# Seven half-width products for eight in an out-projection, with the block sums on GpSimd and inverse sums kept in PSUM

## The chip, the cores and the metric

One core of one Trainium2 chip. The metric is the device time of one execution in microseconds. The trace's span is shorter than that time (246.8 against 248.62 us in the profiled run of the kernel before); times inside an execution are us from the span's start. A run is called slow when its time is over 1.5% above the fastest of the same kernel; ratios use fast runs alone.

## The reference, cut to what matters

```python
# q, k, v: [8, 8, 576, 64], p: [8, 8, 32, 64], w_in: [512, 2048], w_out: [2048, 512]
def sm_attn(qq, kk, vv):                      # softmax(scale q k^T) v
    ...
p_packed = sm_attn(p, k, v)                   # 32 packed rows per head
x = sm_attn(q, p_packed, p_packed)            # -> 4608 tokens x 512
h = x @ w_in
out = (h * np.cos(h)) @ w_out                 # the last product is the out-projection
```

Each of eight batches has 576 tokens: four row blocks of 128 and a half block of 64. Two batches share a fifth block ("joint").

## The kernel before: the parts that the change and the argument touch

One batch is a phase. Its *attention part* computes both softmaxes; its *slot* computes 16 hidden-layer blocks (`h_mm`). Out-projection matmuls of the batch before are a *filler* that `fill(n)` strews between both, so that TensorE never waits for the softmax or for the cosine.

```python
A = ctx.enter_context(tc.tile_pool(name="psA", bufs=3, space=PSUM))   # scores, sums, hidden blocks
O = ctx.enter_context(tc.tile_pool(name="psO", bufs=2, space=PSUM))   # out-projection

def recips(b):                      # two tiny VectorE operations, [128, 2]
    V.reciprocal(r1[b], sums1[b])
    V.tensor_scalar(out=rs1[b], in0=r1[b], scalar1=scale, scalar2=None, op0=ALU.mult)

def sums2(b, y):                    # softmax sums; their logarithm goes to SBUF, which frees psA at once
    if b not in lns:
        lns[b] = att_pool.tile([128, 2, S], FP32, name="lns", tag="lns")
    ps = psa()
    ...                             # two matmuls with ones
    ACT.activation(out=lns[b][:, y]..., in_=ps[:, :, 0:HS], func=AF.Ln)

def h_mm(b, fc):                    # hidden block fc: matmuls, cosine on ScalarE, product on VectorE
    ps = psa()
    ...
    def rest():
        V.tensor_tensor(out=gT[b][:, fc, :]..., in0=ps[:, :, 0:HS], in1=csv, op=ALU.mult)
        if fc % 8 == 7:
            G.tensor_copy(out=joint[b // 2]..., in_=gT[b][:, fc - 7:fc + 1, 512:576])
    return rest

def out_gen(b):                     # 16 matmuls of 512 columns for each row block
    for grp in groups:
        pss = {c: O.tile([128, DM], FP32, name="ot", tag="ot") for c in grp}
        ...
                nc.tensor.matmul(pss[c], w, w_out_bf[:, fc, :], start=(fc == 0), stop=(fc == NFC - 1))
                if fc == NFC - 1:
                    osb = o_pool.tile([128, DM], FP32, name="osb")
                    copy(out_eng[n_out[0] % len(out_eng)], osb, pss[c])

for s in range(3, B):               # attention part, then slot
    fill(1000); set_filler(s - 1)
    if nxt: permute_v(s + 1)        # GpSimd
    s2(s); ppw(s, 2, V); ...
    recips(s + 1)
    xbar("k", s + 2)                # transposing DMA of k
    G.tensor_copy(out=gate, in_=xT["k", s + 2][0:1, 0, 0:1])   # GpSimd waits here until k is transposed
    ...
    for n, b in (("v", s + 2), ("q", s + 2), ("k", s + 3)):
        load(n, b)                  # issued by GpSimd, behind the gate
    slot(s, ...)
```

The softmax here doesn't subtract the row's maximum and nothing guards it: scores larger than these inputs give would overflow.

## Time and profile before

Median 248.38 us of two runs (248.23 to 248.54). The table is worked out from the trace's list of TensorE instructions; a phase runs from the first hidden block of one slot to that of the next.

| | before |
|---|---|
| busy TensorE / VectorE / ScalarE / GpSimd, share of the span | 94 / 67 / 68 / 23 % |
| slot 1 starts, slot 2 starts | 44.2, 77.6 us |
| phases from slot 2 on | 26.1, 25.2, 28.4, 25.2, 28.1 us (64 or 80 whole matmuls of filler in turn) |
| slot 7, then the tail to the end of the span (246.8 us) | 13.4, 22.8 us |

TensorE is full; the others have a third or more of their time free. A change that removes TensorE work should therefore gain, as long as what it puts on the other engines fits between.

### The profile page before, as it was taken

The page shows a single profiled execution, that of the slowest core. Times are in us where ns is not written, and L with a number is a line of the kernel's source. Part 1 is how long each engine was busy: PE and PEld are TensorE (multiplying, and loading weights), DVE is VectorE, ACT ScalarE, POOL GpSimd, SP SyncE. Part 2 cuts the span into 40 slices and gives each one's busy share as a digit, 9 for nine tenths or more (in the row PEclk, how much of TensorE's full clock was granted, in tenths as well). Part 3 has the DMA queues.
Part 4 walks back from the last instruction along what each step waited for, and adds up shares of the span by engine and source line. Part 5 has one row for each costly group of instructions (what it writes and reads, how often), then busy time and mean ns, then how long its engine had stood idle before and what let it go on. Part 6 is the DMA issues. An engine that isn't in the chain of part 4 may idle for free.

```text
span 246.8 us, 5023 instructions
## 1 busy us (share of the span) xinstructions
PE 233.2 (94%) x1996; PEld 130.9 (53%) x2029; DVE 165.2 (67%) x248; ACT 169.0 (68%) x282; POOL 57.7 (23%) x70
## 2 busy tenths in 40 slices
PE   8788799999999999999999999999999999999993
PEld 3454374566545654565446554565456554665452
DVE  3549987677658776678767766678766684886110
ACT  2369799877576787888787776888778684873000
POOL 8342533240400355004503105030500100001000
PEclk9999999999999999999999999999999999999999
DMA  6999999999899999999999997999571113111133
GB/s 90 202 203 206 205 206 228 194 241 151 179 202 184 192 175 214 218 198 142 222 211 187 172 201 91 198 166 171 109 154 27 45 43 84 43 31 57 47 84 85
DMA packets 64231, 37.36 MB, mean 151 GB/s; under 512 B 36848, under 2 KB 59632, under 8 KB 64208
## 3 DMA queue, kind: packets, MB, share of 16 engines
q0 software_dynamic: 23152, 18.75, 50.0%
q1 hardware_dynamic: 40624, 18.09, 35.1%
q8 instruction: 16, 0.26, 0.4%
q10 hardware_dynamic: 432, 0.20, 0.4%
q14 instruction: 7, 0.06, 0.1%
HBM read 37.22 MB, written 9.44 MB: 189 GB/s over the span
## 4 chain that ended last, share of the span: by engine, by line
PE 78%; DMA 12%; issue 2%; DVE 2%; ACT 2%; POOL 2%; DVEq 0%; POOLq 0%
PE ot L309 46%; PE psA L256 21%; DMA vbf<-in_v_dram 10%; PE psA L207 3%; DMA a1T<-a 2%; PE psA L129 2%; PE psA L183 2%; DVE gT L263 2%; PE ot L295 1%; PE psA L233 1%; ACT cosT L260 1%; POOL vp L77 1%; ACT ppT L75 1%; POOL kbf L84 1%; PE ot L104 0%
## 5 line engine op out<-in xcount | busy, mean ns | idle before, releaser
L309 PE MATMUL ot<-w_out_bf,gT 128*128 128x512 bf16 x482 | 127.5, 379 | 2.0 <-issue 1.1
L263 DVE TENSOR_TENSOR gT<-psA,cosT 128x576 bf16<-128x576 f32 x128 | 93.8, 755 | 28.9 <-ACT cosT L260 28.2
L260 ACT ACTIVATE cosT<-psA 128x576 bf16<-128x576 f32 x128 | 82.4, 652 | 24.6 <-PE psA L256 22.1
L256 PE MATMUL psA<-a2n,PPW 128*128 128x288 bf16 x512 | 83.8, 286 | 1.6 <-DVE gT L263 0.4
L309 PEld LDWEIGHTS <-gT 128*128 128x128 bf16 x512 | 47.8, 98 | 43.4 <-issue 6.7
L256 PEld LDWEIGHTS <-PPW 128*128 128x128 bf16 x512 | 49.3, 98 | 34.6 <-issue 3.9
L77 DVE CAST PPW<-psA 128x1024 bf16<-128x1024 f32 (+1 forms) x23 | 26.9, 1175 | 11.6 <-PE psA L207 11.5
L267 POOL COPY joint<-gT 128x512 bf16<-128x512 bf16 x16 | 9.9, 616 | 82.5 <-DVE gT L263 82.5
L77 DVE COPY osb<-ot 128x512 f32<-128x512 f32 (+1 forms) x22 | 14.9, 678 | 17.5 <-PE ot L309 7.7
L77 POOL COPY vp<-vbf 96x3072 bf16<-96x3072 bf16 x7 | 19.3, 2751 | 6.3 <-DMA vbf<-in_v_dram 6.3
L75 ACT COPY osb<-ot 128x512 f32<-128x512 f32 (+1 forms) x15 | 8.5, 567 | 15.3 <-PE ot L309 10.6
L243 DVE SCALAR_TENSOR_TENSOR a2n<-a2u,r,lns 128x576 bf16<-128x576 bf16 x16 | 12.3, 812 | 7.3 <-ACT lns L241 7.3
L235 ACT ACTIVATE lns<-psA 128x576 f32<-128x576 f32 x16 | 10.1, 650 | 7.1 <-PE psA L233 6.5
L140 ACT ACTIVATE a<-psA 128x576 bf16<-128x576 f32 x16 | 10.3, 647 | 6.7 <-PE psA L129 6.7
L309 PE MATMUL ot<-w_out_bf,joint 128*128 128x512 bf16 x47 | 12.8, 379 | 0.1
L225 ACT ACTIVATE a2u<-psA,rs 128x576 bf16<-128x576 f32 x16 | 11.0, 737 | 1.4 <-PE psA L129 1.3
L75 ACT CAST ppT<-psA 64x128 bf16<-64x128 f32 x24 | 6.2, 260 | 7.0 <-DVE ppT L77 5.9
L207 PE MATMUL psA<-w_in_bf,ppT 64*32 64x512 bf16 x224 | 10.1, 380 | 0.0
L241 ACT ACTIVATE lns<-lns 128x576 f32<-128x576 f32 x16 | 10.0, 676 | 0.0
L347 PE MATMUL ot<-wz 128*128 128x512 bf16 x23 | 7.7, 468 | 1.4 <-DVE wz L358 1.2
L527 POOL COPY gate<-kT 1x1 bf16<-1x1 bf16 x3 | 0.5, 181 | 32.3 <-DMA kT<-kbf 32.3
L183 PEld LDWEIGHTS <-vp 96*128 96x128 bf16 x192 | 6.5, 98 | 2.3 <-issue 1.2
(73 smaller groups left out, 152.7 us busy)
## 6 DMA issues: line engine op xcount, KB each, us to landing
kbf<-in_k_dram POOLq DMA_DIRECT2D x8, 576.0 KB, 12.6
vbf<-in_v_dram POOLq DMA_DIRECT2D x8, 576.0 KB, 7.6
qbf<-in_q_dram POOLq DMA_DIRECT2D x8, 576.0 KB, 10.1
out_dram<-osb SPq DMA_DIRECT2D x24, 192.0 KB, 2.7
out_dram<-osb SPq DMA_DIRECT2D x22, 128.0 KB, 2.4
w_in_bf<-in_moe_w_in_dram POOLq DMA_DIRECT2D x4, 512.0 KB, 17.3
w_out_bf<-in_moe_w_out_dram POOLq DMA_DIRECT2D x4, 512.0 KB, 21.2
out_dram<-osb SPq DMA_DIRECT2D x26, 64.0 KB, 2.1
```

Source lines behind the costliest of these rows:

```text
L75: ACT.copy(out=out, in_=in_)
L77: eng.tensor_copy(out=out, in_=in_)
L140: ACT.activation(out=a1[b % 2][:, y, :, 0:TP].rearrange("p (e m) x -> p e m x", e=2), in_=ps[y][:, :, 0:HS].rearrange("p e (m x) -> p e m ...
L183: nc.tensor.matmul(ps[:, hp * 64:(hp + 1) * 64], vp[b][:, c, hp * 128:(hp + 1) * 128], a1T[b][0:TP, :, j, 32 * hp:32 * hp + 32], start=(j ...
L207: nc.tensor.matmul(ps[y][32 * x:32 * x + 32, :], ppT[b % 2][r, 2 * x + y, :], w_in_bf[r, x, n * 512:(n + 1) * 512], start=True, stop=True)
L225: ACT.activation(out=a2u[b][:, y].rearrange("p (e x) -> p e x", e=2), in_=ps[y][:, :, 0:HS], func=AF.Exp, scale=rs1[b][:, y:y + 1])
L235: ACT.activation(out=lns[b][:, y].rearrange("p (e x) -> p e x", e=2), in_=ps[:, :, 0:HS], func=AF.Ln)
L243: V.scalar_tensor_tensor(out=a2n[b][:, y], in0=a2u[b][:, y], scalar=r1[b][:, y:y + 1], in1=lns[b][:, y], op0=ALU.mult, op1=ALU.mult)
L256: nc.tensor.matmul(ps[:, e, 0:HS], PPW[b][:, y, fc * 128:(fc + 1) * 128], a2n[b][:, y, e * HS:(e + 1) * HS], start=(y == 0), stop=(y == 1))
L260: ACT.activation(out=csv, in_=ps[:, :, 0:HS], func=AF.Sin, bias=PI_HALF)
L263: V.tensor_tensor(out=gT[b][:, fc, :].rearrange("p (e x) -> p e x", e=2), in0=ps[:, :, 0:HS], in1=csv, op=ALU.mult)
L309: nc.tensor.matmul(pss[c], w, w_out_bf[:, fc, :], start=(fc == 0), stop=(fc == NFC - 1))
```

## The change

Two row blocks of 128 tokens and the two halves of `w_out` (even and odd hidden chunks, left and right columns) form a 2 by 2 block product. It has eight block products; with sums of blocks formed beforehand and results added afterwards, seven suffice. A matmul of 512 columns is called a *whole*, one of 256 a *half*. Two row blocks together are a *pair*. The sums of `w_out` blocks (T) are formed once, those of the token blocks (S) for each batch.

```diff
+    def T_sums(i, eng):                       # 4 sums of 2048 elements, on VectorE in slot 1
+        in0, in1 = ((B_blk(0, 1), B_blk(0, 0)), (B_blk(1, 1), T[0]), ...)[i]
+        eng.tensor_tensor(out=T[i], in0=in0, in1=in1, op=ALU.subtract)
+    def S_sums(b, p, eng, k0, k1, which=(0, 1, 2, 3)):
+        for i in which:                       # S1 = A21+A22, S2 = S1-A11, S3 = A11-A21, S4 = A12-S2
+            eng.tensor_tensor(out=out, in0=in0, in1=in1, op=op)
+    def pairs_gen(b):                         # replaces the whole matmuls of batches 1 to 7
+        m = {1: (A11, B_blk(0, 0)), 2: (A12, B_blk(1, 0)), 3: (S4, B_blk(1, 1)),
+             4: (A_blk(b, 2 * p + 1, 1, 0, 8), T[3]), 5: (S1, T[0]), 6: (S2, T[1]), 7: (S3, T[2])}
+        ...                                   # 8 matmuls of 256 columns each
+            V.tensor_tensor(out=out, in0=in0, in1=one, op=ALU.add)      # results added out of PSUM
     def slot(s, hooks, keep=0, heavy={}):
         for fc in range(NFC):
             h_mm(s, fc)()
+            if s > 1 and fc in (7, 11):
+                S_sums(s, 0, G, *((0, 4) if fc == 7 else (4, 6)))
+    def close(s, steps=(0, 1)):
+        eng = V if s == B - 1 else G          # the other sums; the last batch's on VectorE
+        ...
     def sums2(b, y):
-        ACT.activation(out=lns[b][:, y]..., in_=ps[:, :, 0:HS], func=AF.Ln)
+        ps = lns[b, y] = psa()                # inverse sums stay in PSUM until the normalising product
+        ACT.activation(out=ps[:, :, 0:HS], in_=ps[:, :, 0:HS], func=AF.Ln)
 for s in range(3, B):
-        fill(1000); set_filler(s - 1)
+        close(s - 1, (0,))                    # S of pair 0 (rest), S1 and S2 of pair 1
         if nxt: permute_v(s + 1)
         ...                                   # gate, loads
+        close(s - 1, (1,))                    # S3 and S4 of pair 1, behind the gate and the loads
         slot(s, ...)
```

The change also has one buffer for the permuted v where there were two, and three for output tiles where there were four.

## The prediction

> **What bounds the kernel now.** I read the page first: busy shares, the chain that ended last, the costliest groups.
>
> ```profile
> PE 233.2 (94%) x1996; PEld 130.9 (53%) x2029; DVE 165.2 (67%) x248; ACT 169.0 (68%) x282; POOL 57.7 (23%) x70
> ...
> PE 78%; DMA 12%; issue 2%; DVE 2%; ACT 2%; POOL 2%; DVEq 0%; POOLq 0%
> ...
> L309 PE MATMUL ot<-w_out_bf,gT 128*128 128x512 bf16 x482 | 127.5, 379 | 2.0 <-issue 1.1
> L263 DVE TENSOR_TENSOR gT<-psA,cosT 128x576 bf16<-128x576 f32 x128 | 93.8, 755 | 28.9 <-ACT cosT L260 28.2
> L256 PE MATMUL psA<-a2n,PPW 128*128 128x288 bf16 x512 | 83.8, 286 | 1.6 <-DVE gT L263 0.4
> ...
> L267 POOL COPY joint<-gT 128x512 bf16<-128x512 bf16 x16 | 9.9, 616 | 82.5 <-DVE gT L263 82.5
> L77 DVE COPY osb<-ot 128x512 f32<-128x512 f32 (+1 forms) x22 | 14.9, 678 | 17.5 <-PE ot L309 7.7
> L77 POOL COPY vp<-vbf 96x3072 bf16<-96x3072 bf16 x7 | 19.3, 2751 | 6.3 <-DMA vbf<-in_v_dram 6.3
> ```
>
> TensorE carries the chain; the out-projection (L309) is its largest group and waited only 2.0 us in all. GpSimd is nearly empty. Busy times of pipelined matmuls overlap, so I took the pitch from two stretches of the chain in order of time where TensorE does nothing else:
>
> ```profile
> 228.37 10.74 PE ot L309 x49
> 239.16 3.67 PE ot L295 x32
> ```
>
> A 512-column matmul (379 ns alone) costs (10.74 - 0.379) / 48 = 215.9 ns; a 256-column one (272 ns alone), with a weight load for each, costs (3.67 - 0.272) / 31 = 109.6 ns. A half is thus 1.6 ns dearer than half a whole, and its 98 ns weight load is just hidden. Last, the busy time by stretch. One batch is a phase of two parts: attention work with out-projection matmuls between it, then a slot of 16 hidden-layer blocks with more of them. Batch 6:
>
> ```profile
> core 0: us, PE busy (x) PEld busy (x) DVE busy (x) ACT busy (x) POOL busy (x), PEclk, DMA share, GB/s
> 182.70:202.20 19.50, 19.28 (x158) 11.48 (x162) 13.93 (x18) 14.60 (x25) 0.77 (x2) 1.00 0.16 44
> 202.20:210.80 8.60, 8.55 (x70) 3.95 (x71) 5.30 (x6) 5.11 (x8) 0.46 (x1) 1.00 0.24 61
> ```
>
> The first line is slot 6, the second the attention part after it. TensorE is full in both, at clock 1.00. VectorE has 5.6 us left in the slot, and that reserve is what the change spends.
>
> **What the Trainium skill says.** (1) "TensorE: Matmul & The Clock Gate", Back-to-back issue gap, gives two figures: an isolated gap of N/2.4 + 2.5 ns and a sustained 131 ns per 512 columns. The trace agrees with the first (216 against 215.9, 109 against 109.6) and not with the second. (2) "GPSIMD Engine Reference", section 3.1, gives about 2.6 cycles at 1.2 GHz per element of a two-input operation and 4497 ns for 2048 fp32 elements. No two-input GpSimd row exists here. Its copies agree with the page's one-input rate: (2751 - 616) / (3072 - 512) = 0.83 ns an element, one cycle. (3) "VectorE: DVE Perf Modes", the perf-mode tier table, gives 1224 ns for a bf16 tensor_tensor of 2048 elements in SBUF; no row here has that form. (4) "SBUF - State Buffer", Who interferes with whom, says that a VectorE instruction with two SBUF inputs contends with GpSimd reads. The old normalising product has two; with the inverse sums in PSUM it has one. The old product takes 812 ns against 755 of the gating product that reads PSUM, so at best 0.06 us each are gained besides the freedom from contention.
>
> **The change part by part.**
>
> *Products.* Each of batches 1 to 7 had 64 whole matmuls for its four row blocks, 13.82 us; now 112 halves, 12.28 us. 7 x 1.54 = 10.8 us saved. The shared fifth blocks of batches 1, 3 and 5 become halves: 96 x 109.6 against 48 x 215.9, 0.16 us lost. Net on TensorE: -10.6 us, all of it on the path as long as TensorE stays fed.
>
> *Sums on GpSimd, batches 1 to 6.* Per batch twelve operations of 512 elements and eight of 256: 8192 elements. Estimate from the skill's 2.6 cycles (2.17 ns an element) and 0.1 us an instruction: 12 x 1.21 + 8 x 0.66 = 19.8 us. To it come the v permutation 2.75, two joint copies 1.2, three load issues 2.3 and a gate 0.5: 26.5 us a batch. TensorE's own phase: the phases starting at 129.0, 157.4 and 182.7 took 28.4, 25.3 and 28.1 us with 80, 64 and 80 whole matmuls; with 128 halves (14.0 us) in each that is about 25.2. So at the skill's rate GpSimd is the longer one, by about 1 us a phase; at 1.9 ns an element (24 us) it would fit. It also has deadlines: the v permutation comes behind the sums, ready about 12.5 us into a phase, and the next use of it (sixth block of the slot) comes at about 13.3 us.
>
> *Evacuations.* Per batch VectorE and ScalarE had 4 or 5 copies of 690 or 581 ns, half on each. Now VectorE does nearly all: per pair two 512-column operations (0.69) and three of 256 (0.42) = 2.64 us, twice, plus about two copies of 0.42: 6.1 us against 1.7 before. Its phase grows from 19.2 (13.93 + 5.30) to about 23.5 of 25.2 us. In the slot, with the ten halves held back, TensorE has 64 halves 7.0 + 16 blocks of 0.49 + 1.4 of other matmuls = 16.2 us, and VectorE 13.2 + about 3 = 16.2 us as well. Neither can lend the other time, and the hidden blocks rotate through three PSUM buffers. I put 0.5 us of slip on each of six slots: +3 us.
>
> *Weight sums in slot 1.* Four VectorE operations of 1.22 us (skill) = 4.9 us in a stretch of 7.3 us in which VectorE is busy 6.4. Most can be absorbed by buffers and by the attention part that follows: +1.5 to +2 us.
>
> *Last batch.* All its sums are on VectorE and stand in its queue before the evacuations: four of 256 elements (about 0.25) and eight of 512 (about 0.4) = 4.2 us. The last gated block is ready about 1.4 us after the slot; with one evacuation between, VectorE reaches the second bank's evacuation at 6.4 us and frees it at 7.1, while TensorE has done its 10 + 8 + 16 + 8 halves by 4.7 us. Stall about 2.3 us; this eats the last batch's 1.5.
>
> *Normalising product.* Queued behind evacuations, its second half comes with only six halves (0.66 us) of cover: up to +0.2 us a phase, +1 in all.
>
> *Sum.* -10.6 + 3 + 1.8 + 2.3 + 1 = -2.5 us with GpSimd just fitting; GpSimd at the skill's rate adds 2 to 5 us over four phases but shares them with the VectorE slip. With everything hidden but the tail stall: about -8 us.
>
> **The rivals.**
>
> *A: TensorE stays the bound.* For it: it is full now, and the ordering of the change (halves of GpSimd sums interleaved, products split, evacuations arranged so that two go in one instruction) looks arranged around exactly these waits. Against it: the VectorE balance of the slot. It gives 248.4 - 8 to -6 = 240 to 242 us.
>
> *B: VectorE becomes the bound of the slots.* For it: 16.2 against 16.2 us and three rotating buffers. Against: before, VectorE's idle time was almost only waiting for ScalarE (28.2 of 28.9 us), and part of its work can slide into the attention part, which has 3 us of reserve. It gives 244 to 246 us.
>
> *C: GpSimd becomes the bound.* For it: 26.5 us of work per phase of 25.2. Against: the rate is a figure for fp32 that nothing here has tested for bf16, and every sum was put there on purpose. It gives 247 to 251 us.
>
> *D: transfers.* Loads are issued behind the sums on the same queue. Before, the gate for them opened 13.4 us after the phase began (133.4 against about 120), held by the transposes of k and not by GpSimd, so a queue that arrives at 13 us loses little. I give it no time of its own.
>
> **Range and chances.** I weigh A at about 0.45, B at 0.35 and C at 0.2. My sum alone would say 246; I lean towards A, since a wait that I counted fully may be covered by TensorE's other matmuls, and because the reordering is so specific. I choose 243.4 us, range 239.5 to 249.0. The 2% limit is 243.4, so faster by over 2% has 0.46, within 2% 0.44, slower 0.10.
>
> **What would show it.** Right: a half-width pitch near 110 ns in the out-projection; GpSimd tensor_tensor rows near 1.2 us for 512 elements and its busy time near 175 us; VectorE busy near 190 us; phases of 25 to 26 us; a stall of about 2 us on TensorE just after the last slot, ended by VectorE. Wrong: if the sums on GpSimd take 0.8 us or less, C falls and A gains; if they take 1.5 us or more, TensorE will wait for S tiles in each phase and the kernel is slower. If the slots run at TensorE's pace with VectorE over 95% busy, my 3 us there were not real. If weight loads show at the 256-column pitch (over 115 ns), the saving itself is smaller: each ns costs 0.9 us.

## The result, and the profile after

The changed kernel takes 268.42 us (267.89 and 268.95, two runs): 8% slower, and outside the predicted range. The ratio to before is 1.0806, 95% interval 1.071 to 1.0903. A ratio here is the mean time of one kernel's fast runs over that of the other's in the same rounds, so it is not quite the ratio of the medians quoted.

The page of the changed kernel: busy times, then the chain that ended last by engine and by line.

```profile
PE 233.7 (87%) x2407; PEld 170.7 (64%) x2413; DVE 200.3 (75%) x327; ACT 164.6 (62%) x278; POOL 177.1 (66%) x198
...
POOL 28%; PE 20%; DVE 7%; DMA 6%; ACT 3%; issue 2%; POOLq 0%; DVEq 0%; ACTq 0%
POOL S L303 23%; PE ot L412 11%; DMA kT<-kbf 6%; PE psA L262 4%; DVE gT L269 4%; PE ot L322 3%; DVE osb L371 2%; ACT cosT L266 2%; POOL joint L273 2%; POOL vbf L87 1%; POOL qbf L87 1%; DVE S L303 1%; ACT ppT L78 1%; PE psA L209 1%; PE psA L186 1%
```

TensorE led the chain with 78%; now GpSimd does with 28%, most of it in the block sums (L303). Yet no engine is full: the fullest is TensorE with 87%. So the loss must lie in waits and not in a saturated engine. TensorE's busy time has not fallen, partly because some of its matmuls ran at half clock (mean granted clock 0.977; h1 below, which has these products in batches 2 to 7 and ran at clock 1.00, has 228.0 us).

Groups of the changed kernel, different shapes kept apart, and last the gate of the kernel before:

```profile
L303 POOL TENSOR_TENSOR S<-gT 128x512 bf16<-128x512 bf16 x38 | 43.4, 1155 | 0.0
L303 POOL TENSOR_TENSOR S<-gT 128x256 bf16<-128x256 bf16 x26 | 17.4, 670 | 0.0
L155 DVE TENSOR_SCALAR rs<-r 128x2 f32<-128x2 f32 x8 | 6.1, 765 | 0.3
L661 POOL COPY gate<-kT 1x1 bf16<-1x1 bf16 x3 | 0.5, 182 | 10.6 <-DMA kT<-kbf 10.6
```

```profile
L527 POOL COPY gate<-kT 1x1 bf16<-1x1 bf16 x3 | 0.5, 181 | 32.3 <-DMA kT<-kbf 32.3
```

The sums take 1155 and 670 ns, where 1.21 and 0.66 us were predicted. The gate is the surprise: GpSimd, the busiest helper of the change, stood 10.6 us in three waits for the transposed k. The wait was there before, 32.3 us long, when GpSimd had nothing else to do and it cost nothing. And a scaling of two elements takes VectorE 765 ns on average.

Where the time came from, phase by phase (starts of the slots' first hidden blocks; experiments included for later):

| kernel | slot 1 | 2 | 3 | 4 | 5 | 6 | 7 | slot 7 ends | span |
|---|---|---|---|---|---|---|---|---|---|
| before | 44.2 | 77.6 | 103.6 | 128.9 | 157.3 | 182.5 | 210.6 | 224.0 | 246.8 |
| after | 49.0 | 87.0 | 115.3 | 141.6 | 167.8 | 201.2 | 227.1 | 242.4 | 267.2 |
| e3_before_psum_only | 48.5 | 83.4 | 108.9 | 134.2 | 162.6 | 187.8 | 215.9 | 229.3 | 252.1 |
| e2_ln0_sbuf | 44.3 | 84.8 | 113.0 | 139.1 | 165.3 | 196.7 | 222.6 | 237.8 | 264.1 |
| e4_sums_before_gate | 48.1 | 86.1 | 114.3 | 140.4 | 166.6 | 192.7 | 218.6 | 233.9 | 260.1 |
| i2_after_b1 | 48.6 | 84.0 | 110.9 | 137.0 | 163.1 | 190.3 | 216.2 | 231.5 | 256.3 |
| g1_all2 | 44.4 | 87.8 | 116.1 | 142.2 | 168.3 | 194.5 | 220.4 | 235.6 | 258.7 |
| g2_small_evac | 44.3 | 87.8 | 114.2 | 138.7 | 164.3 | 189.9 | 215.1 | 229.6 | 251.2 |
| h1_full_b1 | 44.7 | 78.6 | 106.2 | 132.3 | 158.5 | 184.6 | 210.5 | 225.7 | 248.8 |
| i1_h1_small | 44.5 | 78.4 | 104.6 | 130.1 | 155.7 | 181.2 | 206.5 | 220.9 | 242.6 |

Against before, the change loses 4.8 us up to slot 1, 4.6 more up to slot 2, 2.2 up to slot 3, 1.1 up to slot 4 and 8.2 in the phase of slot 5 (33.4 us against 25.2); slot 7 and the tail bring 3.9 more. Only two phases gain, those of slots 4 and 6, by 2.2 us each. Three places in the trace show most of it. The 4.6 us up to slot 2 are lost in attention part 2 (19.9 us against 15.8; slot 1 itself takes 18.1 against 17.6): TensorE waits there 1.4 us for VectorE, 1.2 for a joint copy and 0.6 for block sums.

**Before slot 1.** VectorE's instructions in the prologue, of the kernel before:

```profile
26.59 0.15 DVE L151 RECIPROCAL r<-sums 128x2 f32<-128x2 f32 x1
26.77 0.17 DVE L152 TENSOR_SCALAR rs<-r 128x2 f32<-128x2 f32 x1
```

and of the changed one, with GpSimd's copy of v at the same time (start, duration):

```profile
28.70 0.16 DVE L154 RECIPROCAL r<-sums 128x2 f32<-128x2 f32 x1
28.89 3.10 DVE L155 TENSOR_SCALAR rs<-r 128x2 f32<-128x2 f32 x1
```

```profile
29.20 2.76 POOL L80 COPY vp<-vbf 96x3072 bf16<-96x3072 bf16 x1
```

Batch 0's inverse sums now hold two of the three psA buffers, so TensorE's transposes of k for batch 1 follow one another through the one left. First the kernel before, then two of the three groups after:

```profile
17.54 1.40 PE L104 MATMUL psA<-ident,kbf 96*128 96x96 bf16 x24
```

```profile
19.29 0.50 PE L107 MATMUL psA<-ident,kbf 96*128 96x96 bf16 x8 [0.65 <-DVE kT L80]
20.44 0.50 PE L107 MATMUL psA<-ident,kbf 96*128 96x96 bf16 x8 [0.65 <-DVE kT L80]
```

The scaling comes about 2 us later than before. There it meets GpSimd's copy and ends with it, at 31.96 to 31.99 us: 3.10 us for what took 0.17. (It starts 0.31 us ahead of the copy, while GpSimd still issues a load; in e3 below it starts inside the copy.) TensorE then waits 2.95 us for a gated product, and its next 8 hidden-layer matmuls run at half clock.

**The cycle through the gate.** The chain of waits of the changed kernel in order of time (start, us):

```profile
162.91 6.38 POOL S L303 x7
169.29 0.29 POOL vp L80
169.59 6.78 DMA kT<-kbf
...
176.41 0.18 POOL gate L661
...
176.65 0.79 POOL vbf L87
...
178.22 4.49 POOL S L303 x4
182.71 0.56 POOL joint L273
```

GpSimd forms sums, permutes v, waits at the gate (here 4.44 us idle) for k's transposition, issues the loads and only then forms the last four sums, 4.5 us, which are ready to be formed all the while. The gate opens at 118.33, 146.83 and 176.41: 28.5 and 29.6 us apart, while TensorE's phases take 26.2. GpSimd falls behind by 2.2 to 3.4 us a phase, unnoticed, until TensorE meets it. The transposing DMA itself starts later in each phase too: 2.2 us before slot 3's start, 0.1 before slot 4's, 1.8 after slot 5's. It stands in SyncE's queue behind the transposition of q and output stores. What delays it was not tested.

TensorE's instructions there (start, duration, in brackets the idle time before and what ended it):

```profile
187.27 1.03 PE L322 MATMUL ot<-w_out_bf,joint 128*128 128x256 bf16 x8 [0.46 <-DVE osb L371]
191.07 1.89 PE L322 MATMUL ot<-w_out_bf,joint 128*128 128x256 bf16 x8 [2.76 <-POOL joint L273]
```

TensorE waits 2.76 us for a copy of 0.61 us that stands in GpSimd's queue behind sums which nobody needs yet. Then eight matmuls take 1.89 instead of 1.03 us: the clock has halved, and stays so to 197 us (mean granted clock 0.77 from 186 to 201 us). The Trainium skill, "TensorE: Matmul & The Clock Gate", Part 1, tells of a halved clock after an idle window of about 3.4 us; here it followed idle stretches of 0.46 and 2.76 us with 1.03 us of work between them.

**After the last slot**, TensorE in the changed kernel:

```profile
242.74 1.04 PE L412 MATMUL ot<-w_out_bf,S 128*128 128x256 bf16 x8
246.38 1.92 PE L412 MATMUL ot<-w_out_bf,gT 128*128 128x256 bf16 x16 [2.60 <-DVE osb L371]
```

This stall of 2.60 us is close in length to the 2.3 us that the prediction worked out, but it is not the same stall: it comes right after the halves held back from batch 6, where the prediction had 32 halves of the last batch in between. VectorE there:

```profile
243.94 0.71 DVE L303 TENSOR_TENSOR S<-gT 128x256 bf16<-128x256 bf16 x1
...
245.91 0.94 DVE L371 TENSOR_TENSOR osb<-ot,osb 128x256 f32<-128x256 f32 x2
246.77 0.75 DVE L303 TENSOR_TENSOR S<-gT 128x512 bf16<-128x512 bf16 x2
```

The evacuation that frees the bank, one of batch 6's last, stands behind the four sums of 256 elements alone (243.94 to 245.38 us). The eight sums of 512 follow it, and TensorE waits for none of them. The second line of TensorE also tests the predicted pitch: (1.92 - 0.272) / 15 = 109.9 ns a half, predicted 109.6.

### The profile page after: what moved, and what is told of

Read it like the earlier page. It is cut to its first block, busy times and chain, and to the rows that moved or that the text cites. A ratio compares the mean times of both kernels' runs of the same rounds, so it can differ in the third digit from the quotient of the medians.

```text
span 267.2 us, 6076 instructions
## 1 busy us (share of the span) xinstructions
PE 233.7 (87%) x2407; PEld 170.7 (64%) x2413; DVE 200.3 (75%) x327; ACT 164.6 (62%) x278; POOL 177.1 (66%) x198
## 4 chain that ended last, share of the span: by engine, by line
POOL 28%; PE 20%; DVE 7%; DMA 6%; ACT 3%; issue 2%; POOLq 0%; DVEq 0%; ACTq 0%
POOL S L303 23%; PE ot L412 11%; DMA kT<-kbf 6%; PE psA L262 4%; DVE gT L269 4%; PE ot L322 3%; DVE osb L371 2%; ACT cosT L266 2%; POOL joint L273 2%; POOL vbf L87 1%; POOL qbf L87 1%; DVE S L303 1%; ACT ppT L78 1%; PE psA L209 1%; PE psA L186 1%
## 5 line engine op out<-in xcount | busy, mean ns | idle before, releaser
L266 ACT ACTIVATE cosT<-psA 128x576 bf16<-128x576 f32 x128 | 81.6, 654 | 28.4 <-PE psA L262 24.9
L262 PEld LDWEIGHTS <-PPW 128*128 128x128 bf16 x512 | 49.6, 98 | 26.4 <-issue 12.5
L303 POOL TENSOR_TENSOR S<-gT 128x512 bf16<-128x512 bf16 (+1 forms) x64 | 60.8, 958 | 0.0
L412 PE MATMUL ot<-T,S 128*128 128x256 bf16 x336 | 48.9, 273 | 2.2 <-POOL S L303 2.0
L412 PEld LDWEIGHTS <-S 128*128 128x128 bf16 x448 | 43.1, 98 | 10.8 <-POOL S L303 2.8
L412 PE MATMUL ot<-w_out_bf,gT 128*128 128x256 bf16 x224 | 34.5, 281 | 3.1 <-DVE osb L371 3.1
L303 POOL TENSOR_TENSOR S<-S,gT 128x512 bf16<-128x512 bf16 (+1 forms) x32 | 30.4, 958 | 1.6
L303 POOL TENSOR_TENSOR S<-gT,S 128x512 bf16<-128x512 bf16 (+1 forms) x32 | 30.4, 958 | 0.0
L322 PE MATMUL ot<-w_out_bf,joint 128*128 128x256 bf16 x128 | 16.6, 282 | 6.1 <-POOL joint L273 3.9
L412 PE MATMUL ot<-T,gT 128*128 128x256 bf16 x112 | 16.8, 272 | 1.1 <-DVE osb L371 1.0
L344 PE MATMUL ot<-w_out_bf,gT 128*128 128x512 bf16 x60 | 16.4, 379 | 0.4 <-issue 0.3
L412 PE MATMUL ot<-w_out_bf,S 128*128 128x256 bf16 x112 | 15.8, 272 | 0.0
```

The costliest lines, as they stand in the source:

```text
L262: nc.tensor.matmul(ps[:, e, 0:HS], PPW[b, fc // 4][:, y, fc % 4 * 128:fc % 4 * 128 + 128], a2n[b][:, y, e * HS:(e + 1) * HS], start=(y == ...
L266: ACT.activation(out=csv, in_=ps[:, :, 0:HS], func=AF.Sin, bias=PI_HALF)
L303: eng.tensor_tensor(out=out, in0=in0, in1=in1, op=op)
L322: nc.tensor.matmul(ps, joint[b // 2][:, fc, :], w_out_bf[:, fc, cols], start=(fc == 0), stop=(fc == NFC - 1))
L344: nc.tensor.matmul(pss[c], gT[b][:, fc, c * 128:(c + 1) * 128], w_out_bf[:, fc, :], start=(fc == 0), stop=(fc == NFC - 1))
L412: nc.tensor.matmul(tile_[:, i], lhs[:, kp, :], rhs[:, kp, :], start=kp == 0, stop=kp == 7)
```

## The experiments

Eighteen runs. The theory after reading the two traces was that the loss is a sum: GpSimd's queue (G in the expectations), held PSUM buffers, VectorE's evacuations and the tail. The rival was that one of them carries it alone, GpSimd's added work above all.

### GpSimd's queue

**e1_free_sums** (wrong result): no block sums in batches 1 to 6; the products read plain blocks.

```diff
-        if (b, p) not in S:
+        if (b, p) not in S and b == B - 1:
+        if b < B - 1:
+            return
```

> The changed kernel without the block sums of batches 1 to 6: their products read blocks of gT directly, so GpSimd has no sums there. The result is wrong on purpose; all matmuls, evacuations and the last batch's sums stay. Theory G (GpSimd falls behind, 28.5 us a batch against 26.2 us of TensorE, and TensorE pays where it catches up): the 8.1 us lost in the phase from 167.8 to 201.2 go, and 2 to 3 us of waits for S and joint in the second batch's attention part; 256 to 259 us. Rival V (VectorE is the bound of the slots): at most 2 us less, 266 to 268 us.

Measured: 261.81 us, ratio 1.0521 (1.049 to 1.0553), 6.6 us below the change. One of its four runs took 582 us, and that was the profiled one; its hidden-layer matmuls took 576 ns on average against 289 in the change, so its trace tells nothing of the waits. The gain fell short of what was expected: with no sums at all, two thirds of the loss remain. GpSimd is one cause of several.

**e4_sums_before_gate**: nothing but the place of the last four sums, ahead of the gate instead of behind the loads.

```diff
+            close(s - 1, (1,))
             if s + 2 < B:
                 xbar("k", s + 2)
                 G.tensor_copy(out=gate, in_=xT["k", s + 2][0:1, 0, 0:1])
...
-        close(s - 1, (1,))
         slot(s, ...)
```

> The changed kernel with the last two sums of the second pair placed in GpSimd's queue ahead of the gate that waits for the transposed k, not behind the loads. Theory G, refined: GpSimd stands idle 2.8 to 4.4 us a batch at that gate while 4.5 us of sums wait behind it; filled, its batch falls from 28.5 to about 25.5 us, it keeps up, and the 8.1 us wait at 187 to 191 us with the half clock after it goes: 259 to 262 us. Rival: the rate of the sums is the bound, not their order: 266 us or more. Loads start about 1 us later, which should not matter.

Measured: 261.61 us, ratio 1.053 (1.0477 to 1.0582), the same as with no sums at all. The phase of slot 5 takes 26.2 instead of 33.4 us. GpSimd's waits from 100 to 200 us, first of the change, then of this run (total us, times, longest):

```profile
POOL gate L661 <- DMA kT<-kbf: 10.6, 3, 4.4
```

```profile
POOL gate L663 <- DMA kT<-kbf: 0.2, 1, 0.2
```

With the same work, GpSimd hardly waits: the sums fill the time of the transposing DMA. So in the phases from slot 2 on it was the order of GpSimd's work that cost 6.8 us, and not its amount: TensorE does not wait for GpSimd there any more. The two waits in attention part 2 (1.2 and 0.6 us) are unchanged.

### Inverse sums in PSUM

**e3_before_psum_only**: the kernel before with this one part of the change.

```diff
-            lns[b] = att_pool.tile([128, 2, S], FP32, name="lns", tag="lns")
-        ps = psa()
+        ps = lns[b, y] = psa()
...
-        ACT.activation(out=lns[b][:, y]..., in_=ps[:, :, 0:HS], func=AF.Ln)
+        ACT.activation(out=ps[:, :, 0:HS], in_=ps[:, :, 0:HS], func=AF.Ln)
```

> The kernel before with this part of the change alone: inverse sums in PSUM in all batches, the product not split. Theory P: slot 1 starts 2 us later by the lack of PSUM buffers, up to 4.7 us if the small VectorE operation meets the GpSimd copy again; later batches keep their length. 250 to 253 us. Rival: the loss at the start comes from other parts of the change (buffers merged, order of loads), 248 to 249 us.

Measured: 254.05 us, ratio 1.022 (1.0189 to 1.0252), correct. One part, meant as a small gain for VectorE, costs 5.7 us alone. The table shows where: 4.3 us up to slot 1, 1.5 more up to slot 2, nothing later. VectorE and TensorE in this run:

```profile
29.65 2.19 DVE L152 TENSOR_SCALAR rs<-r 128x2 f32<-128x2 f32 x1
```

```profile
32.56 2.08 PE L255 MATMUL psA<-a2n,PPW 128*128 128x288 bf16 x8 [2.04 <-DVE gT L262]
```

The scaling is again caught by the copy of v (29.05 to 31.81 us), and TensorE idles 2.04 us and then runs at half clock (eight matmuls in 2.08 us; undisturbed blocks of four start 0.49 us apart).

**e2_ln0_sbuf**: the change with batch 0's inverse sums in SBUF.

```diff
+        if b == 0:
+            if y == 0:
+                ln0.append(s_pool.tile([128, 2, SQ], FP32, name="lns0", tag="S1"))
+            lns[b, y] = ln0[0][:, y].rearrange("p (e x) -> p e x", e=2)
...
```

> The changed kernel with the inverse sums of batch 0 alone in SBUF as before; those of the other batches stay in PSUM. Theory P (two of three PSUM buffers held in the prologue make transposes of k wait for one, and the 2 us of delay push a small VectorE operation into a GpSimd copy that blocks it): slot 1 starts at 44.4 us again instead of 49.0 and the time falls by 4 to 5 us, to about 264. Rival G: GpSimd's queue sets the later pace whatever the start, since it waits for transfers; the gain is lost again and the time stays above 267.

Measured: 265.59 us, ratio 1.0693 (1.0666 to 1.0721). Slot 1 starts at 44.3 us, so the prologue's 4.7 us are recovered in full; but slot 2 starts only 2.3 us earlier than in the change. 2.8 us are left of the gain: in attention part 2 TensorE now waits 2.7 us for a joint copy, where it waited 1.2.

### Weight sums, tail and scaling

**f1_T_early**: the four weight sums still on VectorE, two in attention part 1, two in attention part 2.

```diff
-             (7, tk("k", 2, 2)), (7, lambda: T_sums(0, V)), ... (14, lambda: T_sums(3, V))], 8, {3: 3})
+             (7, tk("k", 2, 2)), (9, lambda: pack_p(2, 4)), (12, next_loads)], 8, {3: 3})
```

> The changed kernel with its four weight sums moved out of slot 1, still on VectorE: one each behind the first and second PPW casts of batch 1's attention part (the second behind the normalising products), two in batch 2's attention part. Theory T (these 4.9 us stall the slot, which took 21.5 us against 17.6 before): slot 1 is back near 18 us, part of it returns in batch 2's attention part; net 2 to 3 us, so 265 to 266.5. Rival: the slot is long for other reasons (the 1.5 us late transposes, the gate), or GpSimd's pace takes the gain: above 267.5.

Measured: 267.53 us, ratio 1.077 (1.0737 to 1.0803). A miss: moving them within VectorE gains 0.9 us, no more than the change's own two runs differ. The premise was misread: slot 1 took 18.1 us in the change and not 21.5, so there were not 2 to 3 us to win in it.

**f2_tail**: the last batch's pair-1 sums between the evacuations.

```diff
-    close(B - 1)
+    S_sums(B - 1, 0, V, 6, 8)
+    S_sums(B - 1, 1, V, 0, 8, ())
+    set_filler(B - 1)
+    fill_halves(32)
+    for i in (0, 1, 2, 3):
+        S_sums(B - 1, 1, V, 0, 8, (i,))
+        fill_halves(8 if i in (0, 2) else 0)
```

> The changed kernel with the last batch's sums for its second pair placed on VectorE between the evacuations of the first pair, not ahead of them (and as whole operations of 1024 elements). Theory: the 2.6 us for which TensorE stood still at 243.8 to 246.4 us goes, 265.5 to 266.5. Rival: VectorE's work only moves and TensorE waits later for S2 of the second pair: above 267.5.

Measured: 265.86 us, ratio 1.0674 (1.0596 to 1.0752), but from 263.8 to 269.8 and with a profile of the slow state. The time is inconclusive; the stop is not. It is still 2.60 us in this trace, and as long in f3 and f4 below, fast runs with the same edit. f3:

```profile
238.70 3.53 PE L418 MATMUL ot<-w_out_bf,gT 128*128 128x256 bf16 x16 [2.60 <-DVE osb L377]
```

The edit moved the eight sums of 512 elements, which were not in the way. In g1 and h1, where batch 6's evacuations go ahead of the four sums of 256 as well, the stop is 1.05 us.

**f3_all**: e2, e4, f1 and f2 together.

> All four repairs at once: batch 0's inverse sums in SBUF, the two sums ahead of the gate, weight sums out of slot 1, the last batch's sums between evacuations. If the four losses are separate their gains add: 2.8 (measured) + 6.8 (measured) + 2.5 + 2 = 14 us, 253.5 to 256. If GpSimd's or VectorE's pace is the one bound behind all of them, the sum is clearly smaller: 258 or more. To be faster than before (248.4) it would need the slots at TensorE's pace as well.

Measured: 262.77 us, ratio 1.0573 (1.0549 to 1.0596): no better than e4 alone. Gains of 2.8, 6.8 and 0.9 us measured one at a time do not add. The trace shows two reasons: slot 1 starts at 46.8 us and not at 44.3 as in e2, since the first weight sum now stands on VectorE ahead of the normalising product (TensorE waits 2.3 us for it), and the stop in the tail is as long as before.

**f4_all_rs**: f3 with the scaling on ScalarE, where it takes 203 ns on average (in g1) against VectorE's 765 ns in the change.

```diff
-        V.tensor_scalar(out=rs1[b], in0=r1[b], scalar1=scale, scalar2=None, op0=ALU.mult)
+        ACT.activation(out=rs1[b], in_=r1[b], func=AF.Copy, scale=scale)
```

> The same as the one with all repairs, and the small scaling of the reciprocal sums (2 elements, SBUF to SBUF) on ScalarE in place of VectorE, where it took 765 ns on average against 231 before, because a running GpSimd instruction holds it up. Six batches by about 0.6 us of VectorE time: if VectorE's queue there is on the path, 1 to 3 us less than the other; if not, within 0.7 us of it.

Measured: 261.86 us, ratio 1.054 (1.0501 to 1.0578), 0.9 us below f3. The intervals overlap and the gain lies between both forecasts: not settled.

### VectorE's evacuations

**g1_all2**: five repairs: inverse sums of batches 0 and 2 in SBUF, sums ahead of the gate, weight sums on GpSimd in batch 1, the tail's sums behind the evacuations of batch 6, scaling on ScalarE.

> After with five repairs: inverse sums of batches 0 and 2 in SBUF, the last two block sums of a batch ahead of the gate for the loads, the weight sums on GpSimd in batch 1 while it is idle, the last batch's sums between its evacuations, and the two-element scaling on ScalarE. Theory T (the loss outside the slots is PSUM held in two places, GpSimd's queue and the tail): 251 to 256 us; slot 1 starts near 44.3 and slot 2 near 79 us, later phases 26.2 us each. Rival V (VectorE alone paces the whole kernel, whatever is repaired elsewhere): 260 us or more, as the run with three of these repairs gave. If slot 2 still starts after 83 us, the loss of attention part 2 is neither the held PSUM nor the weight sums.

Measured: 261.21 us, ratio 1.051 (1.0477 to 1.0542). The expected 251 to 256 failed, and this was my own doing. TensorE's one long wait in attention part 2, and GpSimd's queue there:

```profile
72.13 0.61 PE L328 MATMUL ot<-w_out_bf,joint 128*128 128x256 bf16 x2 [7.18 <-POOL joint L279]
```

```profile
67.47 4.06 POOL L295 TENSOR_TENSOR T<-w_out_bf,T 128x2048 bf16<-128x2048 bf16 x1
71.47 0.61 POOL L279 COPY joint<-gT 128x512 bf16<-128x512 bf16 x1
```

A weight sum takes GpSimd 4.06 us, and I had put the last one ahead of the joint copy. Apart from that phase this kernel serves as the base for the next.

**g2_small_evac** (wrong result): g1 with every evacuating addition on VectorE cut to 16 columns; the stores send zeros of full size.

```diff
-            V.tensor_tensor(out=out, in0=in0, in1=one, op=ALU.add)
+            V.tensor_tensor(out=out[..., 0:16], in0=in0[..., 0:16], in1=one[..., 0:16], op=ALU.add)
```

> The kernel with the five repairs, and every evacuating addition of the pair products on VectorE cut from 256 or 512 columns to 16 (wrong result on purpose; the stores send tiles of zeros of the same size). Theory T with rival B of the prediction (VectorE's work for the evacuations slows the slots and attention parts by about 1 us a phase): 5 to 9 us below the kernel with the five repairs, and steady phases of 25.0 to 25.3 us, TensorE's own pace, instead of 26.2. Rival P (the slots are slow for another reason, such as the PSUM rotation of the half-width tiles or TensorE's own pitch): within 2 us of the kernel with the five repairs, phases 26 us.

Measured: 253.2 us, ratio 1.02 (1.0162 to 1.0238): 8.0 us below g1, where 5 to 9 were expected. VectorE's evacuations are a cause in their own right. (For the test the result tiles are fixed ones, zeroed once, and the output tiles have two buffers for three.) The steady phases are 25.6 us (expected 25.0 to 25.3), against 26.2.

### One pair for two, and batch 1

**g4_one_pair_rs**: only the first pair of row blocks by seven products, in the attention part; the second by whole matmuls in the slot, copied by ScalarE. Inverse sums in SBUF, weight sums as in g1, scaling on ScalarE.

```diff
-            return [(0, (1,)), (0, (2, 6)), (0, (7,)), (0, (4, 5)), (None, (3, 1)),
-                    (1, (2, 6)), (1, (7,)), (1, (4, 5)), (1, (3,))]
+            return [(0, (1,)), (0, (2, 6)), (0, (7,)), (0, (4, 5)), (0, (3,))]
...
+        yield from direct(b, ((2,), (3,)))
```

> Only the first pair of row blocks of each batch by seven products, and it in the attention part where VectorE has time; the second pair by eight, in the slot, evacuated by ScalarE as before; inverse sums in SBUF; weight sums on GpSimd in batch 1; scaling on ScalarE. TensorE saves 7 x 0.77 = 5.4 us at most. GpSimd's sums halve (to about 9.5 us a batch). If VectorE in the slots and GpSimd's queue are what cost the change its gain: 243 to 248 us, phases of 25.7 to 26.2 us, and no wait of TensorE for GpSimd over 0.3 us. If 249 to 253: the pairs cost VectorE more in the attention part than they give. Over 254: theory T lacks a cause.

Measured: 258.22 us, ratio 1.0392 (1.0361 to 1.0422). By the expectation "theory T lacks a cause"; the trace shows the same wait of 7.3 us for the joint copy as in g1, which was then known to be mine. The steady phases were 25.7 to 26.2 us, as expected.

**h1_full_b1**: g1 with batch 1 by plain products, and the last weight sum behind slot 1's joint copy.

```diff
-    for k0, k1 in ((0, 4), (4, 6)):
-        S_sums(1, 0, G, k0, k1)
+    T_sums(3, G)
...
-        if b == 0:
+        if b < 2:
```

> The kernel with the five repairs, and batch 1 by plain products (no block sums in it; the weight sums on GpSimd: one ahead of the v permutation, two behind it, the last after slot 1's joint copy). Theory: attention part 2 was slow because batch 1's weight sums and block sums stood before the joint copy and the products that need them. Then slot 2 starts near 77.6 us as before, the phases after it stay at 26.1 us, and the time is 249 to 252 us (1.5 us of TensorE's saving given up). Rival: if slot 2 still starts after 82 us, the loss of attention part 2 lies in VectorE or PSUM there.

Measured: 249.7 us, ratio 1.0035 (1.0019 to 1.0051), correct. Slot 2 starts at 78.6 us (77.6 expected), the steady phases take 26.1 to 26.2 us. All but a microsecond of the loss of 20 us is repaired, but nothing of the 9 us that TensorE saves is seen.

**i1_h1_small** (wrong result): h1 with the additions cut to 16 columns, edited as g2.

> h1 (all repairs, batch 1 plain) with VectorE's evacuating additions cut to 16 columns (wrong result on purpose). Ledger: TensorE's saving without batch 1 is 9.0 us, so 248.4 - 9.0 = 239.4 us if nothing else is lost. Theory (VectorE's evacuations are the rest): 240 to 243 us, that is 7 to 10 us below h1's 249.7, slots and attention parts at 25.5 us. If over 244.5: a further cause is missing from the ledger.

Measured: 244.63 us, ratio 0.9843 (0.9824 to 0.9862), 5.1 us below h1; 7 to 10 were expected, and the time is just over the 244.5 us above which, by the same expectation, a further cause is missing. It is the same test as g2 without g1's accident, so 5.1 us is the size to trust for the repaired kernel. One phase of both, slot and attention part, first h1, then i1 (columns: stretch, length, then busy us of TensorE, its weight loads, VectorE, ScalarE, GpSimd; granted clock, DMA share, GB/s):

```profile
132.30:147.80 15.50, 15.27 (x159) 12.26 (x157) 13.80 (x22) 12.24 (x23) 15.01 (x16) 1.00 1.03 174
147.80:158.45 10.65, 10.20 (x129) 8.18 (x128) 8.21 (x14) 8.04 (x14) 10.41 (x13) 1.00 1.08 185
```

```profile
130.12:145.60 15.48, 15.25 (x159) 12.26 (x157) 12.30 (x22) 12.33 (x22) 15.32 (x16) 1.00 1.03 176
145.60:155.68 10.08, 10.08 (x129) 8.13 (x128) 6.74 (x14) 7.98 (x14) 10.00 (x13) 1.00 1.10 182
```

The slot is 15.5 us in both: taking 1.5 us from VectorE there changes nothing, TensorE sets its length. The attention part loses 0.57 us. Its wait is named by TensorE's waits in h1 between 105 and 210 us:

```profile
PE ot L328 <- DVE osb L377: 1.9, 4, 0.5
```

Once a phase TensorE waits half a microsecond for the PSUM bank of its joint half, which VectorE's additions of the pair before hold. These 0.6 us in four phases are 2.4 of the 6.2 us between the two traces. Another 1.5 lie in slot 2's phase, where h1 waits 1.4 us for block sums, and 2.1 in slot 7 and the tail. Note also GpSimd in i1: 25.3 us busy in a phase of 25.6, and TensorE does not wait for it once in these two stretches.

**i2_after_b1**: the change with batch 1 by plain products and the weight sums on GpSimd, nothing else.

> The changed kernel with one thing undone: batch 1 by plain products, so no block sums in it, and the weight sums on GpSimd where it is idle. If batch 1's sums cost what its attention part lost (19.9 us against 15.8 before): 263 to 266 us, slot 2 starting at 82.5 to 84 us instead of 87.0. If GpSimd's queue in the later batches takes the gain back: 267 us or more, although slot 2 starts early.

Measured: 258.86 us, ratio 1.0435 (1.0398 to 1.0471): 9.6 us below the change, more than expected. 3.0 us come up to slot 2, 1.3 in the phase of slot 2, and 6.2 in the phase of slot 5 (27.2 against 33.4 us). The stall that e4 removed by order is here nearly gone without it: TensorE meets GpSimd only with waits of 0.46 and 0.79 us. GpSimd has no head start (its copy of v begins 2.5 us before slot 3, 1.4 before slot 4 and 1.8 after slot 5; in the change 2.5 and 0.9 before and 1.4 after). What differs is the third gate wait, 0.58 us for 4.44: the transposing DMA of k was issued 0.2 us before slot 5 and not 1.8 after it. Why is not shown. So e4 and i2 remove the same stall in two ways, and their gains would not add.

### Looking for a version that gains

**h2_one_b1**: g4 with batch 1 plain, as in h1.

> One pair of row blocks a batch by seven products in batches 2 to 7, batch 1 plain as above. TensorE saves 6 x 0.77 = 4.6 us. The run with one pair had phases of 26.0 us, TensorE's own pace for that mix, so with attention part 2 repaired: slot 2 starts near 77.6, 244.5 to 247.5 us, ratio 0.985 to 0.997, which would beat the kernel before. If over 249: attention part 2 is not repaired.

Measured: 248.79 us, ratio 1.0004 (0.9989 to 1.002). A miss by more than a microsecond; TensorE still waits 1.2 us for the first block sums in attention part 3, and its saving of 4.6 us is not seen in the time.

**h3_full_act**: h1 with the hidden weights' second evacuation, the joint halves' copies and the first product's copy on ScalarE; no halves held back in the last slot.

```diff
-            copy(out_eng[0], osb, ps)
+            copy(ACT, osb, ps)
...
-            then = {1: lambda ps: copy(out_eng[0], m1, ps), ...
+            then = {1: lambda ps: copy(ACT, m1, ps), ...
```

> The kernel of h1 with a part of VectorE's work on ScalarE: the second hidden-weight evacuation in the slot, the joint halves' copies and the first product's copy; the last slot holds back no halves. If VectorE is what keeps the phases at 26.1 us: phases 25.5 us, 3 to 5 us below h1, 245 to 248 us. If ScalarE becomes the wait (it stands on the softmax chain): no better than h1, within 1 us or above it.

Measured: 250.73 us, ratio 1.0091 (1.0072 to 1.0109), 1.0 us above h1, as the rival had it. The joint half's wait is the same to the digit, 1.9 us in four waits: it is for the additions, which stayed on VectorE. The copies that moved were not in its way. What made it slower than h1 was not found: its phases take 26.4 us where h1's take 26.2, and TensorE's waits in them are the same.

**h4_one_act**: h2 with the two copies of h3.

> The kernel of h2 with the joint halves' copies and the first product's copy on ScalarE also in the attention part. TensorE is full in its phases, so VectorE's relief should be worth little: within 0.7 us of h2. If it is more than 1.5 us below h2, VectorE still cost the one-pair kernel something.

Measured: 247.68 us, ratio 0.9965 (0.9953 to 0.9977). 1.1 us below h2, more than expected; 0.8 of it lies in slot 2's phase, where TensorE's wait for the first block sums is 0.4 us for 1.2. It is the fastest correct version: 0.35% faster than before, with an interval that leaves out 1, though the same by the limit of 2%.

**i3_one_joint**: h4 with one joint half moved ahead of batch 2's pair.

```diff
-        if b == 1:
-            return [(1, 0), (1, 1)]
-        return [(b - (b + 1) % 2, (b + 1) % 2)] if 2 < b < B - 1 else []
+        return [(b - (b + 1) % 2, (b + 1) % 2)] if 0 < b < B - 1 else []
```

> h4 (one pair a batch, ScalarE takes the small copies) with the second joint half of batch 1 moved into batch 2's attention part, ahead of its pair, so that the first block sums have 1.8 us more before TensorE asks for them. If the 1.2 us wait for S was only a matter of place: 246.2 to 247.2 us, 0.6 to 1.2 below h4, ratio to before about 0.992. If the wait is merely pushed to VectorE or the next gate: 247.5 us or more.

Measured: 248.01 us, ratio 0.9978 (0.9957 to 1.0), no better than h4. The expected gain was read from h2's wait of 1.2 us; in h4 it was 0.4. The wait for S is gone, and another stands in its place:

```profile
105.47 0.41 PE L265 MATMUL psA<-a2n,PPW 128*128 128x288 bf16 x2 [0.94 <-DVE a2n L248]
```

## Why the prediction was wrong, point by point

The steps that failed are the prices of three waits. Rival C compared GpSimd's work with TensorE's phase as totals, and rival D gave the gate "no time of its own": the gate's place in the queue alone cost 6.8 us (e4). "Up to +0.2 us a phase, +1 in all" for the inverse sums kept in PSUM: 5.7 us in the kernel before (e3). And "+1.5 to +2 us" for the weight sums, nothing for the block sums of batch 1: 4.3 us up to slot 3 (i2).

The prediction took 10.6 us off TensorE and added 8.1 us of losses; this sum alone said 246 us, and it chose 243.4. The losses were 268.4 - (248.4 - 10.6) = 30.6 us. Taken away one after the other (the order matters, since the runs share a stall):

| step | us | from | predicted |
|---|---|---|---|
| pairs and weight sums in batch 1 (6.2 of it at slot 5) | 11.1 | i2: 9.6, and it does without 1.5 us of the saving | 1.8 |
| inverse sums in PSUM, gate order, tail, scaling | 9.2 | i2 to h1 | 3.3 (tail 2.3, product 1), gate 0 |
| VectorE's evacuating additions | 5.1 | h1 to i1 | 3 |
| not settled | 5.2 | i1 to 248.4 - 9.0 = 239.4 | 0 |

**Products.** Right: the pitch is 109.9 ns, and with small additions the steady phases take 25.6 us where 25.2 was expected. The saving on TensorE is real; it was eaten.

**GpSimd's work.** The durations were right within 5%, in part because two errors cancel: 1.89 ns an element for 2.17, and about 0.18 us an instruction for 0.1. 25.3 us a phase (i1) is within 5% of the 26.5 predicted, in which a gate counts 0.5 us; that is the time of three, one takes 0.18. What failed is the reading of the total. The prediction said that "a queue that arrives at 13 us loses little". But GpSimd's queue is in order: the gate stops it some 3.5 us a batch (10.6 in three), and what stands behind the gate waits too. A total that fits in the phase fits no longer with a wait inside it (28.5 us), and the lag grows in silence until it surfaces as one stall with a halved clock behind it. e4 shows this alone: same work, other order, -6.8 us.

**Batch 1.** The term for the weight sums in slot 1, +1.5 to +2 us, counted VectorE's 4.9 us (each measured at 1.22 us, as predicted). Its 6.4 us of busy VectorE in a stretch of 7.3 are not found: in the 7.3 us from 54.7 to 62.0, the end of slot 1, the kernel before has 5.6. The slot grew by 0.5 us; the loss is in the attention part behind it, where batch 1's block sums come in, for which the prediction had no term of its own. i2 shows both together, 4.3 us up to slot 3 and 6.2 us at slot 5; how much of the 4.3 is the weight sums alone is not settled (f1: moving them within VectorE gains 0.9).

**Normalising product.** The term "up to +0.2 us a phase, +1 in all" was worked out from the product's cover. The cost lay in the buffers: two of three psA buffers held for some microseconds. e3 measures 5.7 us in the kernel before, all of it up to slot 2; the later batches there lose nothing by it. The link to the held scaling, and to the halved clock, was in no step. And the gain for which it was done is small: the product takes 809 ns in e3 against 812, where 60 ns at best were expected.

**Evacuations.** The direction was right, the size (3 against 5.1) and the place were not: "0.5 us of slip on each of six slots" is 0.0 us in the slot and 0.6 in the attention part, where a bank is waited for, and the rest lies in slot 2's phase, slot 7 and the tail. (The 28.9 us that rival B's counterargument reads as VectorE's idle time stand before the gated products alone; VectorE was idle for 81.6 us.) h3 shows that it can't be cured with the copies that ScalarE can take.

**Tail.** 2.60 us against 2.3, which was luck. The prediction counted 4.2 us of sums ahead of the last batch's evacuations; the stop came earlier, behind 1.4 us of them, and f2, which moved the others, left it at 2.60.

**Signs.** The pitch, the length of the sums, GpSimd's busy time (177.1 us, 175 forecast) and a stall in the tail came as the prediction had named them for the case that it was right. None of them bears on the order of a queue or on held buffers, so they could not tell.

**What stays open.** In i1 TensorE's waits from 60 us on add up to 3.5 us (1.7 of it for gated products), against 1.2 in the kernel before. So these waits explain 2.3 of the 5.2 us at most; the other 2.9 were not traced. The rival that came nearest was C, GpSimd, with 247 to 251 us: it had one of the engines right and the mechanism, too much work, wrong.

## What to carry to other kernels

When work is moved to an idle engine, draw its queue in order with the waits in it, not only its sum: a wait for something else (here a gate for loads) lengthens the period of the whole queue, and ready work must stand ahead of it. A buffer kept a little longer can be paid in another stage than the one that was looked at (here the prologue). A stall of the predicted length may be another stall: look at what ends it. And repairs measured one at a time need not add, when two of them remove the same stall (e4 and i2) or one of them is put in the way of another (f1 in f3), so test them together too.

## What the Trainium skill lacked or had wrong

- "TensorE: Matmul & The Clock Gate", Back-to-back issue gap: the sustained 131 ns for 512 columns was not reached in any run; streams run at 215.9 ns before and at 109.9 ns for 256 columns after, as its formula for isolated gaps says.
- The same page, Part 1: it ties the halved clock to an idle window of about 3.4 us, which runs free of the kernel. Here single stops of 2.04 (e3) and 2.95 us (the change) were followed by matmuls at half pace, while the stop of 2.60 us in the change's tail was not (the same stop in e4 and f3 was: 16 matmuls in 2.77 and 3.53 us after it, against 1.92).
- "GPSIMD Engine Reference", section 3.1, has a two-input figure for fp32 alone (4497 ns for 2048 elements). In bf16 the runs show 4.06 us for 2048, 1155 ns for 512 and 670 ns for 256 elements: (4060 - 1155) / 1536 = 1.89 ns an element, 2.27 cycles at the page's 1.2 GHz and not 2.6.
- "SBUF — State Buffer", Who interferes with whom, tells of the lock between VectorE and GpSimd and that the instruction which comes second is blocked whatever its shape. e3 agrees: the scaling began 0.60 us into the copy, and both end together. What the page lacks is a tiny instruction: this one of two elements took 2.19 us (e3) and 3.10 us (the change) for 0.17; on ScalarE it takes 203 ns.
- No page was found to work through the largest single loss here (6.8 us): an in-order queue with a wait in the middle, whose period grows past that of the engine it serves (28.5 against 26.2 us) without any engine being full.
